# One new hand-written order of all operations, and tap products that take the two halves of the array in turn, in a state-space and MLP kernel

## The chip, the cores and the metric

The kernel runs on one core of a Trainium2 chip. Its engines are TensorE (PE in the profile, with its weight loads as PEld), VectorE (DVE), ScalarE (ACT), GpSimd (POOL) and SyncE (SP), which here only issues transfers. The metric is the device time of one execution in microseconds. Where several runs are given, their median counts.

## The reference

One sequence of 2048 positions and 512 channels goes through a long convolution and then through an MLP, each behind a layer norm and with a residual. Cut to what matters:

```python
dt = jnp.exp(log_dt)[:, None]
A = A_re + 1j * A_im; Bc = B_re + 1j * B_im; Cc = C_re + 1j * C_im
P = jnp.exp((dt * A)[:, :, None] * l[None, None, :])          # 512 channels, 128 states, 2048 taps
K = jnp.einsum("dn,dnl,dn->dl", Cc, P, dt * Bc).real
...
y = irfft(rfft(pad(u)) * rfft(pad(K)))[:L] + u * Dskip        # the convolution, by channel
h = x + y                                                     # u is the normed x
h2 = h + (gelu(layernorm(layernorm(h)) @ w1 + b1) @ w2 + b2)  # 512 -> 1376 -> 512
```

The tap index `l` is rounded to bfloat16, so that only some of its values are different from one another in the upper part of the range.

## The kernel before

**The filter.** The 2048 taps of K are made from two tables: a table A for 20 offsets and a table B for 33 multiples of eight, each of them with a real and an imaginary part, for 128 states (the partitions) and 512 channels in four blocks c of 128. The exponentials come from ACT (L793 for B, L991 for A), the sines and cosines from ACT too (L1026 for B, L1063 for A), with angles that PE adds up in PSUM (L1018, L1058, L1061), and DVE multiplies the two (L1036, L1043, L1068). Then `kgen` sums over the states on PE: **the tap products, L1092**. A product has 128 rows, 52 weight columns (two channels of 20 offsets with a gap of 12) and 66 moving columns (two channels of 33). For each step `i` there are four: `Ar` by `Br` and `Ai` by `Bi`, which add up in the same place of PSUM, for t = 0, in the left half of the array's columns (tile position (0, 0), output partitions from 0), and for t = 1, in the right half ((0, 64), partitions from 64). Each block has 32 steps, so there are 512 tap products in all. They read both tables with a step of four elements (`free(..., [[4, ...]])`). A copy from PSUM (`evac`) follows each group of 14 or 4 steps.

**The convolution and the MLP.** Further products on PE turn the taps and the input into a spectrum: `kspec` and `kspec1` (L1120, L1145), `austage` (L946) on the normed input, `fstage` (L967, of which `xspec` for the second half of the sequence is followed by a sum on DVE, L971), `ktail` and `klate` (L1166, L1187). `inverse` multiplies spectra on DVE (L1235) and goes back with PE (L1245), a copy, and a transposing transfer. `tail` adds the residual and does the norms (L1319, L1322, L1323, L1334), and `mlp` has the two matrix products (L1362 with its gelu on ACT in L1364, L1378 with the sum and the residual on DVE in L1380), for four quarters of the sequence. Each finished tile of the output leaves in two transfers from L632, and the very last tile in the program is split in two pieces of 256 columns.

**What sets the order.** Nothing is scheduled when the program is built. `add` records every operation with the engines that it may run on and what it depends on. `ORDER` (L292) is a list of 914 numbers, found beforehand by a search: each is twice the operation's index, plus one where it runs on the second of its possible engines. `Sched.run` (L390) walks the list, takes the eight PSUM slots as the string `SLOTS` says, and emits the operations in that order on each engine's queue, and each engine works its queue from the front. `evac` (L616 on ACT, L618 on DVE) is the main operation that may go to either engine; the row scaling by a norm (L931, L933; L1334, L1336) is another. A transfer may be issued by SP or ACT. A negative number in the list stands for a filler: four matmuls of 128 by 128 with the identity (L1451), into a free PSUM slot. The search used a cost for each operation; the one that stands in the code for a tap step is `add("PE", 0.064 * (hi - lo), ...)`, in microseconds.

Of the kernel before, what the change touches and what calls it, by code (L numbers as in the profile page):

```python
# [275 lines left out]
class VS(V):  # L276
# [13 lines left out]
LAG = {"PE": 0.12, "ACT": 0.20, "DVE": 0.14, "POOL": 0.15, "SP": 0.15}  # L290
OWN = {"PE": 0.0, "ACT": 0.17, "DVE": 0.11, "POOL": 0.1, "SP": 0.0}
ORDER = [  # L292
# [35 lines left out]
]  # L328
SLOTS = "0124626046204620462406220246200626224606446426424602606426042060242042604206246240264024604620406240245651620426262341302560134076205472541326036260721452042067563414307136506437056253104574107423"


TURN = 450000
# [108 lines left out]
def kernel(ctx, tc, A_u, A_A_re, A_A_im, A_B_re, A_B_im, A_C_re, A_C_im, A_log_dt, A_Dskip,  # L441
# [36 lines left out]
    def pst(p, dt=f32):  # L478
        a = banks[:, 512 * p.slot:512 * (p.slot + p.n)]
        return a if dt == f32 else a.bitcast(dt)  # L480
# [76 lines left out]
    def free(off, dims):  # L557

        a = ar[:, 0:1]
        return bass.AP(a.tensor, a.offset + off, [list(a.ap[0])] + dims)  # L560
# [515 lines left out]
    def kgen(c, pr):  # L1076
# [3 lines left out]
        for grp in KIS:  # L1080
            S.pr = pr + 0.01 * KIS.index(grp)
            p = Ps(n=len(grp))
            first = True
            for nb, (i0, n) in enumerate(grp):
                for lo, hi in ((0, n // 2), (n // 2, n)):
                    def fn(e, p=p, nb=nb, i0=i0, lo=lo, hi=hi):
                        for i in range(lo, hi):
                            for t in range(2):
                                q, f = 16 * t + 2 * ((i0 + i) // 4), (i0 + i) % 4
                                o = pst(p)[64 * t:64 * t + 32 + NA, 512 * nb + 2 * NB * i:512 * nb + 2 * NB * i + 2 * NB]  # L1090
                                for ta, tb in ((Ar, Br), (Ai, Bi)):
                                    pe.matmul(o, lhsT=free(ta.lo // 2 + q * 4 * NP_ + f, [[4, NP_ + NA]]), rhs=free(tb.lo // 2 + q * 4 * NB + f, [[4, 2 * NB]]), start=ta is Ar, stop=ta is Ai, tile_position=(0, 64 * t))  # L1092
                    add("PE", 0.064 * (hi - lo), fn, r=[Ar, Br, Ai, Bi], w=[p], new=[p] if first else [])
                    first = False
            i0, n = grp[0]
            N = len(grp)

            def ofn(i0=i0, n=n, N=N):
                return ks().rearrange("p z k i -> p (z k) i")[:, :, i0:i0 + n * N].rearrange("p q (b i) -> p q b i", b=N)

            def ifn(p=p, n=n, N=N):
                return pst(p).rearrange("p (b q) -> p b q", b=N)[:, :, 0:2 * NB * n].rearrange("p b (i q) -> p q b i", q=2 * NB)
            evac(ofn, ifn, 2 * NB * n * N, [p], [kg])
# [397 lines left out]
```

## Time and profile before

| | |
|---|---|
| median of 3 runs | 230.77 us (230.6 to 230.82) |
| the profiled execution | 230.71 us, its span 228.9 us |
| busy in the span: PE, PE's weight loads | 196.2 us (86%), 113.6 us (50%) |
| busy in the span: DVE, ACT, POOL | 173.5 us (76%), 164.4 us (72%), 14.6 us (6%) |
| instructions | 6859 |
| chain that ended last, by engine | PE 53%, ACT 26%, DVE 10%, DMA 4%, issue 4% |

The profile is of one execution, so the working is made against 230.71 us, of which 1.81 us lie outside the span. The two largest groups on PE are the matrix products of the MLP (L1362 40.1 us and L1378 39.8 us busy), and the tap products have 18.3 us. Busy time of PE counts a matmul from its start to its modelled end, so overlapping and waiting matmuls both look busy; starts that follow one another tell more.

### The profile page before, as it was taken

How to read it: one execution, taken by the hardware profiler on the slowest of the kernel's cores; microseconds unless marked ns; L12 is line 12 of the kernel's file. 1: busy time of each engine (PE TensorE's matmuls, PEld its weight loads, DVE VectorE, ACT ScalarE, POOL GpSimd, SP SyncE). 2: the span in 40 equal slices, each digit the busy share in tenths (PEclk: the TensorE clock that was granted, in tenths of full speed). 3: DMA queues.
4: the chain of work that ended last, by engine and by line, in shares of the span. 5: the costliest groups of instructions: out<-in, count | busy, mean ns of one | idle time of the engine just before them, and what ended most of it. 6: DMA issues, size and time to landing. Idle time of an engine off the chain costs nothing.

```text
span 228.9 us, 6859 instructions
## 1 busy us (share of the span) xinstructions
PE 196.2 (86%) x2974; PEld 113.6 (50%) x2981; DVE 173.5 (76%) x279; ACT 164.4 (72%) x203; POOL 14.6 (6%) x26
## 2 busy tenths in 40 slices
PE   7113886776999899999999769999999999999993
PEld 4102752233874479756566446654444434444452
DVE  7999778999897995779899989899957467113022
ACT  4999999999888997998997598593325405803800
POOL 2000300300010001200000030300000101000000
PEclk9999999999999999999999999999999999999998
DMA  5970191153006955486698991019340142051202
GB/s 154 191 145 6 53 234 41 51 159 127 6 3 118 227 145 146 131 180 158 175 243 164 258 227 67 3 33 218 72 93 21 29 101 69 11 126 44 63 21 70
DMA packets 43159, 25.09 MB, mean 110 GB/s; under 512 B 30197, under 2 KB 40697, under 8 KB 43130
## 3 DMA queue, kind: packets, MB, share of 16 engines
q1 hardware_dynamic: 41576, 22.72, 44.2%
q10 hardware_dynamic: 1554, 1.93, 2.7%
q8 instruction: 23, 0.38, 0.7%
q14 instruction: 6, 0.05, 0.1%
HBM read 14.13 MB, written 5.28 MB: 85 GB/s over the span
## 4 chain that ended last, share of the span: by engine, by line
PE 53%; ACT 26%; DVE 10%; DMA 4%; issue 4%; POOL 1%; ACTq 0%; SPq 0%; DVEq 0%; POOLq 0%
PE ps L1362 17%; PE ps L1378 17%; ACT ar L616 8%; PE ps L1092 7%; ACT ar L793 7%; ACT ar L1063 5%; ACT ar L991 4%; PE ps L1245 4%; DVE ar L1235 2%; DMA HL_d<-ar 2%; PE ps L946 2%; DMA ar<-AKc_d 2%; DVE ar L971 1%; DVE ar L1068 1%; ACT ar L701 1%
## 5 line engine op out<-in xcount | busy, mean ns | idle before, releaser
L616 ACT CAST ar<-ps 128x1024 bf16<-128x1024 f32 (+3 forms) x73 | 62.4, 917 | 10.8 <-PE ps L1245 5.3
L1364 ACT ACTIVATE ar<-ps,ar 128x512 bf16<-128x512 f32 (+1 forms) x44 | 27.6, 685 | 34.1 <-PE ps L1362 28.6
L1362 PE MATMUL ps<-ar 128*128 128x512 bf16 (+1 forms) x176 | 40.1, 379 | 0.1
L1378 PE MATMUL ps<-ar 128*128 128x512 bf16 (+3 forms) x181 | 39.8, 366 | 0.3
L1380 DVE TENSOR_TENSOR ar<-ps,ar 128x512 bf16<-128x512 f32 (+1 forms) x17 | 10.6, 652 | 26.7 <-issue 19.7
L1378 PEld LDWEIGHTS <-ar 128*128 128x128 bf16 (+1 forms) x187 | 17.9, 98 | 19.7 <-issue 0.7
L1362 PEld LDWEIGHTS <-ar 128*128 128x128 bf16 (+1 forms) x176 | 17.3, 100 | 20.2 <-issue 0.5
L618 DVE CAST ar<-ps 128x1024 bf16<-128x1024 f32 (+4 forms) x18 | 19.5, 1091 | 6.6 <-PE ps L1092 2.5
L1235 DVE TENSOR_TENSOR ar<-ar 128x2048 bf16<-128x2048 bf16 x20 | 24.0, 1218 | 0.5 <-ACT ar L616 0.3
L1245 PE MATMUL ps<-ar 64*128 64x128 bf16 x672 | 21.5, 216 | 1.9 <-DVE ar L1235 1.5
L1245 PEld LDWEIGHTS <-ar 64*128 64x128 bf16 x672 | 19.1, 94 | 6.5 <-issue 3.2
L1063 ACT ACTIVATE ar<-ps 128x1024 bf16<-128x1024 int16 x20 | 19.5, 1037 | 1.6 <-PE ps L1061 1.4
L1092 PE MATMUL ps<-ar 128*52 128x66 bf16 x512 | 18.3, 242 | 0.4 <-DVE ar L1068 0.4
L689 POOL TENSOR_TENSOR ar<-ar 128x4 f32<-128x4 f32 (+1 forms) x6 | 9.5, 1577 | 143.3 <-DVE ar L694 104.6
L1092 PEld LDWEIGHTS <-ar 128*52 128x52 bf16 x512 | 16.8, 128 | 2.7 <-issue 1.8
L946 PE MATMUL ps<-ar 128*32 128x512 bf16 x256 | 16.4, 381 | 1.0 <-DVE ar L931 0.9
L1026 ACT ACTIVATE ar<-ps 128x1024 bf16<-128x1024 int16 x16 | 15.9, 1035 | 0.4 <-PE ps L1018 0.3
L793 ACT ACTIVATE ar<-ar 128x1024 bf16<-128x1024 f32 x16 | 15.6, 1044 | 0.6 <-DVE ar L675 0.6
L1061 PE MATMUL ps<-ar 128*32 128x256 f16 (+1 forms) x256 | 12.9, 301 | 3.0 <-ACT ar L1063 2.8
L694 DVE SCALAR_TENSOR_TENSOR ar<-ar 128x4 f32<-128x4 f32 (+3 forms) x33 | 9.9, 305 | 6.4 <-POOL ar L689 5.4
L967 PE MATMUL ps<-ar 128*64 128x128 bf16 (+2 forms) x160 | 13.6, 298 | 0.9 <-ACT ar L616 0.9
L1068 DVE TENSOR_TENSOR ar<-ar 128x1024 bf16<-128x1024 bf16 x20 | 12.9, 682 | 0.6 <-ACT ar L1063 0.4
(83 smaller groups left out, 229.0 us busy)
## 6 DMA issues: line engine op xcount, KB each, us to landing
ar<-in_A_u_dram SPq DMA_DIRECT2D x16, 128.0 KB
ar<-in_A_u_dram SPq DMA_DIRECT2D x8, 256.0 KB
out_dram<-ar SPq DMA_DIRECT2D x30, 64.0 KB
ar<-in_B_w_dram SPq DMA_DIRECT2D x3, 344.0 KB
AK_d<-ar SPq DMA_DIRECT2D x2, 512.0 KB
AKc_d<-ar SPq DMA_DIRECT2D x4, 256.0 KB
ar<-tab_TP SPq DMA_DIRECT2D x1, 768.0 KB
ar<-AKc_d SPq DMA_DIRECT2D x3, 256.0 KB
```

The source lines that it names most:

```text
L616: act.copy(out_fn(), in_fn())
L618: dve.tensor_copy(out_fn(), in_fn())
L793: add("ACT", c_act(1024) + 0.03, lambda e, e0=e0: act.activation(free(EB0 // 2 + 4 * (16 - e0), [[8 * e0, 2], [4 * NB, NCH * CW // 4], [1, ...
L946: pe.matmul(pst(p)[32 * j:32 * j + 32, 512 * z:512 * z + 512], lhsT=BX.ap()[:, f0 + z, 16 - 16 * c:48 - 16 * c], rhs=src[2 * j + c].ap(), ...
L1026: add("ACT", c_act(1024), lambda e, p=p, sc=sc, cs=cs: act.activation(sc[cs].ap().rearrange("p c e d -> p (c e d)").rearrange("p (x e f) - ...
L1063: add("ACT", c_act(1024), lambda e, sc=sc: act.activation(sc.ap().rearrange("p z a b -> p (z a b)").rearrange("p (x a f) -> p a x f", a=4, ...
L1092: pe.matmul(o, lhsT=free(ta.lo // 2 + q * 4 * NP_ + f, [[4, NP_ + NA]]), rhs=free(tb.lo // 2 + q * 4 * NB + f, [[4, 2 * NB]]), start=ta is ...
L1235: dve.tensor_tensor(pq.ap().rearrange("p n d -> p (n d)"), a, b_, ALU.mult)
L1245: pe.matmul(pst(p)[:, 512 * h + 128 * k:512 * h + 128 * k + 128], lhsT=q.ap()[rows, x, :], rhs=TP[w].ap()[rows, f0 // 2 + k, :], start=(n ...
L1362: pe.matmul(pst(p)[:fs], lhsT=w1s[dc].ap()[:, fc * P:fc * P + fs], rhs=ybuf.ap().rearrange("p (t c) k -> p c t k", c=4)[:, dc], start=(dc ...
L1364: add("ACT", c_act(512, 1), lambda e, p=p, fc=fc, fs=fs: act.activation(hT.ap()[:fs, fc, :], pst(p)[:fs], ACT.Gelu_apprx_tanh, bias=b1_sb. ...
L1378: pe.matmul(pst(p)[:, c0:c1], lhsT=hT.ap()[:fs, fc, 128 * t:128 * t + 128], rhs=w2s[fc].ap()[:fs, c0:c1], start=(fc == 0), stop=(fc == NFC ...
```

## The change

Three things are changed, and the set of operations stays as it is: the same 914 operations with the same work and the same dependencies.

1. `ORDER` and `SLOTS` are replaced. (One row of the table stands for all.)
2. One filler, `-4`, stands in the new list: four matmuls with the identity into slot 3, between the transposed copies of L840 and the products of L865.
3. In `kgen`, the loop over the two halves is now inside the loop over the real and the imaginary part: the products go left, right, left, right where they went left, left, right, right.

```diff
 ORDER = [
-    2, 0, 52, 4, 58, 54, 56, 50, 62, 154, 6, 64, 66, 68, 74, 82, 8, 102, 104, 12, 10, 136, 194, 14, 140, 106, 88, 108, 16, 24, 32, 118, 100, 60, 28,
...
+    52, 0, 54, 6, 8, 2, 4, 10, 50, 64, 102, 62, 154, 12, 66, 68, 82, 76, 136, 98, 140, 70, 282, 104, 106, 86, 16, 78, 192, 14, 138, -4, 108, 118, 92,
...
                     def fn(e, p=p, nb=nb, i0=i0, lo=lo, hi=hi):
                         for i in range(lo, hi):
-                            for t in range(2):
-                                q, f = 16 * t + 2 * ((i0 + i) // 4), (i0 + i) % 4
-                                o = pst(p)[64 * t:64 * t + 32 + NA, 512 * nb + 2 * NB * i:512 * nb + 2 * NB * i + 2 * NB]
-                                for ta, tb in ((Ar, Br), (Ai, Bi)):
-                                    pe.matmul(o, lhsT=free(ta.lo // 2 + q * 4 * NP_ + f, [[4, NP_ + NA]]), rhs=free(tb.lo // 2 + q * 4 * NB + f, [[4, 2 * NB]]), start=ta is Ar, stop=ta is Ai, tile_position=(0, 64 * t))
+                            for ta, tb in ((Ar, Br), (Ai, Bi)):
+                                for t in range(2):
+                                    q, f = 16 * t + 2 * ((i0 + i) // 4), (i0 + i) % 4
+                                    o = pst(p)[64 * t:64 * t + 32 + NA, 512 * nb + 2 * NB * i:512 * nb + 2 * NB * i + 2 * NB]
+                                    pe.matmul(o, lhsT=free(ta.lo // 2 + q * 4 * NP_ + f, [[4, NP_ + NA]]), rhs=free(tb.lo // 2 + q * 4 * NB + f, [[4, 2 * NB]]), start=ta is Ar, stop=ta is Ai, tile_position=(0, 64 * t), skip_group_check=True)
                     add("PE", 0.064 * (hi - lo), fn, r=[Ar, Br, Ai, Bi], w=[p], new=[p] if first else [])
```

The order of the instructions moves on every engine. Three places matter for what follows.

**ACT, at the end of the sines of table A for the blocks c = 2 and 3** (L1063; `ps` is PSUM, `ar` the one large SBUF tile). The rows `128x66x14` and `128x66x4` are the copies of tap products, 14 or 4 steps each. Before:

```order
L1063 ACTIVATE ar<-ps 128x4x64x4 x4
L616 CAST ar<-ps 128x1024
L1063 ACTIVATE ar<-ps 128x4x64x4
L616 CAST ar<-ps 128x1024
L616 CAST ar<-ps 64x2x9x32
L1063 ACTIVATE ar<-ps 128x4x64x4
L616 CAST ar<-ps 128x1024 x4
L616 CAST ar<-ps 128x66x14
```

Now:

```order
L616 CAST ar<-ps 64x2x9x32
L1063 ACTIVATE ar<-ps 128x4x64x4
L616 CAST ar<-ps 128x1024 x2
L1063 ACTIVATE ar<-ps 128x4x64x4
L616 CAST ar<-ps 128x1024
L1063 ACTIVATE ar<-ps 128x4x64x4
L616 CAST ar<-ps 128x66x14
L1063 ACTIVATE ar<-ps 128x4x64x4
L616 CAST ar<-ps 128x66x14
L616 CAST ar<-ps 128x66x4
```

The first copy of block 2's tap products stood behind the last sine and four other copies; now it stands ahead of the last sine, so that block 2's tap products are on PE before block 3's sines are done. On PE, eight of the 16 `austage` and `xspec` groups of the first half of the sequence stood before the very first tap product; now eleven do.

**DVE, from the scaling of the second half's rows (L931) to the first products of `inverse` (L1235).** Before:

```order
L931 TENSOR_SCALAR ar<-ar 128x512 x2
L618 CAST ar<-ps 128x2x8x32
L931 TENSOR_SCALAR ar<-ar 128x512 x4
L1235 TENSOR_TENSOR ar<-ar 128x2048
L618 CAST ar<-ps 128x4x2x128
```

Now:

```order
L931 TENSOR_SCALAR ar<-ar 128x512
L618 CAST ar<-ps 128x66x14
L618 CAST ar<-ps 128x66x4
L1104 TENSOR_TENSOR ar<-ar 128x2x32
L1235 TENSOR_TENSOR ar<-ar 128x2048
L618 CAST ar<-ps 64x2x9x32
L618 CAST ar<-ps 128x1024
```

Copies of tap products that ACT did there are DVE's now. Over the list up to the first product of the MLP, DVE has 24 evacuations where it had 18, and ACT 69 where it had 75. Of DVE's six more, four are of 128x1024, one is of 128x924, and the sixth is the balance of smaller ones. DVE gives up one L931, two L1323 and one L1334 by the same point, which ACT does or which come later.

**SP, the last transfers of the program** (64 rows of the output each). Before:

```order
L632 DMA out_dram<-ar 64x512 x16
L632 DMA out_dram<-ar 64x256
L632 DMA out_dram<-ar 64x512 x2
L632 DMA out_dram<-ar 64x256
```

Now:

```order
L632 DMA out_dram<-ar 64x512 x12
L632 DMA out_dram<-ar 64x256
L632 DMA out_dram<-ar 64x512 x4
L632 DMA out_dram<-ar 64x256
L632 DMA out_dram<-ar 64x512 x2
```

The tile that is finished last was the second 256-column piece, whose two transfers left one from SP and one from ACT; now it is a whole tile of 512 columns, and both of its transfers leave from SP, one behind the other.

More of the change, by code (lines that the diff above doesn't have):

```diff
@@ L292 @@
 ORDER = [
[35 rows of a table removed]
[35 rows of a table added]
 ]
-SLOTS = "0124626046204620462406220246200626224606446426424602606426042060242042604206246240264024604620406240245651620426262341302560134076205472541326036260721452042067563414307136506437056253104574107423"
+SLOTS = "0124602642046204620240600602402624606041624020402062062046240240624026404062402460462024024062460260462102406710223421367242604132470176354620021601043072547124356403401576471540234614020321756474"
 TURN = 450000
```

68 rows, old and new, of the table ORDER are left out of this document.

## The prediction

> **What bounds the kernel now.** I read the stages first: the busy time of each engine in windows cut where the chain of waits changes its engine. Columns: the stretch, its length, then PE, its weight loads, DVE, ACT and POOL, busy us with counts.
>
> ```profile
> 0.00:119.30 119.30, 94.52 (x2046) 60.29 (x2048) 105.13 (x168) 109.96 (x126) 8.76 (x22) 1.00 0.54 128
> ...
> 25.00:47.00 22.00, 16.74 (x342) 9.29 (x338) 18.48 (x35) 21.93 (x24) 4.12 (x8) 1.00 0.39 99
> 47.00:57.00 10.00, 7.66 (x166) 3.81 (x154) 9.62 (x14) 9.52 (x11) 0.00 (x0) 1.00 0.48 152
> 57.00:69.40 12.40, 12.33 (x340) 9.72 (x344) 11.19 (x16) 10.84 (x13) 0.89 (x2) 1.00 0.02 4
> 69.40:80.00 10.60, 9.51 (x200) 4.75 (x196) 9.44 (x14) 10.05 (x12) 0.00 (x0) 1.00 0.94 182
> 80.00:94.50 14.50, 14.48 (x380) 11.98 (x378) 10.97 (x26) 12.57 (x16) 2.16 (x2) 1.00 0.48 134
> 94.50:119.30 24.80, 24.17 (x556) 14.88 (x557) 22.35 (x30) 23.16 (x28) 0.00 (x0) 1.00 0.80 190
> 119.30:140.70 21.40, 17.44 (x404) 12.79 (x400) 20.41 (x32) 16.62 (x22) 1.93 (x1) 1.00 0.86 198
> 140.70:225.40 84.70, 84.20 (x535) 40.50 (x539) 47.51 (x81) 37.84 (x56) 3.94 (x3) 1.00 0.30 63
> ```
>
> From 140.7, where the first product of the MLP starts, PE is busy 84.20 of 84.70 us: from there the end is fixed by PE's own work. So the question is when the MLP starts, and what stands behind 225.4. Ahead of 140.7 no one engine is the bound. ACT is full from 25 to 47, and DVE from 119.3 on. In between, the chain of waits (start, us, what) changes hands:
>
> ```profile
> 57.07 2.33 PE ps L1092 x66
> ...
> 69.47 1.03 ACT ar L1063
> ...
> 85.11 4.16 PE ps L1092 x120
> ...
> 94.53 0.59 ACT ar L616
> ```
>
> From 57 to 69.4 and from 80 to 94.5 it lies on PE, mostly on tap products; between them it lies on the sines of blocks 2 and 3 on ACT, and PE waits. Who waits for the taps says the list of waits (us in total, times, longest):
>
> ```profile
> DVE ar L618 <- PE ps L1092: 2.5, 2, 1.5
> ACT ar L616 <- PE ps L1092: 2.0, 4, 1.0
> DVE ar L618 <- PE ps L1145: 1.7, 1, 1.7
> ```
>
> **The turned tap products: nothing.** Do the halves already work at once? I looked at short windows of L1092 alone, where the count is of matmuls in flight, then of L967, whose 128-column products go left and right by turns in the program, and of L1254, whose products use the whole array.
>
> ```profile
> 57.06:57.08 0.02, 0.01 (x2) 0.01 (x2) 1.00 0.00 0
> 57.13:57.15 0.02, 0.02 (x4) 0.02 (x5) 1.00 0.00 0
> ...
> 57.06:59.40 2.34, 2.33 (x68) 2.16 (x68) 1.00 0.03 7
> ...
> L1092 PE MATMUL ps<-ar 128*52 128x66 bf16 x512 | 18.3, 242 | 0.4 <-DVE ar L1068 0.4
> ```
>
> ```profile
> 105.60:105.62 0.02, 0.02 (x2) 0.02 (x4) 1.00 0.61 218
> 105.62:105.64 0.02, 0.02 (x4) 0.02 (x6) 1.00 0.58 218
> ```
>
> ```profile
> 122.00 0.68 PE L1254 MATMUL ps<-ar 128*128 128x128 bf16 x9 [0.19 <-ACT ar L616]
> ...
> L1254 PE MATMUL ps<-ar 128*128 128x128 bf16 x16 | 1.1, 220 | 0.2 <-ACT ar L616 0.2
> ```
>
> Products on one and the same tile start one by one: L1254's nine in 0.68 us, (0.68 - 0.22) / 8 = 57 ns apart, never two within 20 ns. Taps start two within 20 ns, then two more by 57.13 to 57.15, some 65 ns later, and L967 likewise goes from two in flight to four. In the program the first two taps are both left ones, so I read the pair as one left and one right product: the array serves each half from its own queue and already overlaps them. Their rate, less the last one's own 0.24, is (2.33 - 0.24) / 67 = 31.2 ns a product, so each half takes 62 ns for 66 columns. What is slow is then each half by itself; the loads speak for the reading with a step of four elements as the cause:
>
> ```profile
> L1092 PEld LDWEIGHTS <-ar 128*52 128x52 bf16 x512 | 16.8, 128 | 2.7 <-issue 1.8 <-DVE ar L1068 0.6
> L967 PEld LDWEIGHTS <-ar 128*64 128x64 bf16 x160 | 6.9, 110 | 5.0 <-issue 3.3
> ```
>
> 52 stepped columns load in 128 ns, 64 plain ones in 110. Turning the order changes no reading, so I take 0. The bound below: the nearest row of products in turn,
>
> ```profile
> 122.99:125.10 2.11, 1.96 (x64) 1.79 (x64) 1.00 0.40 94
> ...
> L1245 PE MATMUL ps<-ar 64*128 64x128 bf16 x672 | 21.5, 216 | 1.9 <-DVE ar L1235 1.5 <-ACT ar L616 0.4
> ```
>
> L1245, has (1.96 - 0.22) / 63 = 27.6 ns a product: 512 x 3.6 = 1.8 us less PE work. A loss I exclude: L967 and L1245 pay nothing for turning.
>
> [...]
>
> **The new order, up to the MLP.** Two moves take PE work out of the stretches where PE is the chain. Three more groups of `austage` and `xspec` stand ahead of the first tap product, in 47 to 57, where PE has 2.3 us idle; and block 2's 128 tap products (128 x 31.2 = 4.0 us) are ready for PE before the last sines, where PE waits. So the copies that wait late for PE's results come sooner: I count DVE's waits for L1092 and L1145, 2.5 + 1.7 = 4.2 us, as gone. A third: DVE has one more early evacuation, which can fill its hole in 25 to 47 (22.0 - 18.48 = 3.5 us idle). The rows of these:
>
> ```profile
> L618 DVE CAST ar<-ps 128x1024 bf16<-128x1024 f32 x10 | 12.0, 1219 | 2.4 <-ACT ar L991 1.2 <-PE ps L967 0.9 <-PE ps L1120 0.3
> L618 DVE CAST ar<-ps 128x924 bf16<-128x924 f32 x3 | 3.4, 1118 | 2.5 <-PE ps L1092 2.5
> L618 DVE CAST ar<-ps 128x512 bf16<-128x512 f32 x2 | 1.4, 692 | 1.7 <-PE ps L1145 1.7
> L931 DVE TENSOR_SCALAR ar<-ar 128x512 bf16<-128x512 bf16 x16 | 5.6, 406 | 0.1
> L1323 DVE BATCH_NORM_STATS2 ar<-ps 128x6 f32<-128x512 f32 x4 | 2.5, 680 | 0.0
> L1334 DVE TENSOR_SCALAR ar<-ps,ar 128x512 bf16<-128x512 f32 x2 | 1.5, 804 | 0.0
> ```
>
> That gives 4.2 + 1.2 = 5.4 us less idle on DVE. Against it stands what DVE takes over from ACT: four copies of 1219, one of 1118 and a balance of about 0.4 make 6.4 us, less the scalings and statistics that it gives up (0.41 + 2 x 0.68 + 0.80 and two small ones of some 0.15: 2.9): 3.5 us more by the start of the MLP. Net 3.5 - 5.4 = **-1.9 us**. The cost is laid on DVE because it has the least air in 119.3 to 140.7 (20.41 of 21.40); ACT, with 16.62, gives those copies up, and takes the load of the gelu table earlier, under 1.3 us that it can bear.
>
> The ends of this term: DVE is idle 9.7 us between 47 and 140.7 (0.38 + 1.21 + 1.16 + 3.53 + 2.45 + 0.99). If all of it went, and the early copy filled its hole too, the term were 3.5 - 9.7 - 1.2 = -7.4; if none went, +3.5. I stay near the named waits, since the rest of DVE's idle is spread over waits under 1.5 us.
>
> **The filler and SP's queue: nothing.** Four matmuls in front of L865:
>
> ```profile
> PE ps L865 <- DVE ar L675: 9.4, 2, 8.7
> ...
> L840 PE MATMUL ps<-ar 128*128 128x128 bf16 x16 | 2.1, 285 | 0.0
> ...
> SPq L1261 <- DVE ar L1334: 24.9, 2, 15.2
> ```
>
> L865 waits 9.4 us for DVE there. L840's sixteen of the same size take (2.1 - 0.285) / 15 = 121 ns each, so the filler is 0.5 us, which it would cost if that wait were gone. The transfers and transposes that change places on SP wait longest for DVE's results (24.9 us for the two transposes of L1261), not for a place in the queue; up to the last ones I cost them at 0. One that waits for a late result would hold those behind it, up to the 15.2 us of the longest such wait; that belongs to the slower rival.
>
> **The end.** The last instructions before:
>
> ```profile
> 225.39 0.42 DVE L1380 TENSOR_TENSOR ar<-ps,ar 128x256 bf16<-128x256 f32 x1 [0.52 <-PE ps L1378]
> ...
> 225.42 1.23 SPq L632 DMA_DIRECT2D out_dram<-ar  x2
> ...
> L1380 DVE TENSOR_TENSOR ar<-ps,ar 128x512 bf16<-128x512 f32 x15 | 9.7, 683 | 24.3 <-issue 19.7 <-PE ps L1378 4.4 <-DMA out_dram<-ar 0.2
> ```
>
> SP issues a transfer in 1.23 / 2 = 0.6 us. The last sum took 0.42 us, and its transfer waited until SP was done with the one before, so the second issue ended 1.26 us after the sum's start. Now the sum takes 0.68 and two issues follow on one queue: 0.68 + 2 x 0.61 = 1.90. That is **+0.64 us**, with nothing to hide it; between +0.26 (only the sum) and +0.9.
>
> **Sum:** 230.71 - 1.9 + 0.64 = 229.45, say **229.5 us**. The profiled execution is within 0.06 of the median, 230.77.
>
> **The rivals.**
>
> *The halves do not overlap before* (0.14). Then turning halves the taps: 512 x 15.6 = 8.0 us less on PE between 57 and 94.5. For it: L1245 streams 128 columns in 2 x 27.6 = 55 ns a half, by which 66 would take 28.5, near the 31.2; against it: the paired starts. PE leaves the chain there, and DVE becomes the bound; of its other 9.7 - 4.2 = 5.5 us idle half would go, so 229.5 - 2.75 = 226.7.
>
> *DVE becomes the bound* (0.27), the case on the slower side. In 94.5 to 140.7 it is busy 42.76 of 46.2 us, and the new list puts copies of tap products there just ahead of L1235. If they stand in its queue ahead of products that PE, ACT and a transposing transfer wait for, DVE's idle only changes place. It decides where less than 3.5 + 0.64 = 4.1 of the hoped 5.4 us goes. With half of the 4.2 left, 3.5 - 3.3 + 0.64 = +0.8, 231.5; with all of it, 3.5 - 1.2 + 0.64 = +2.9, 233.6. I take 231.9.
>
> *It comes out even* (0.13): the list was sought with costs that differ from the chip's elsewhere, and the middle wins no more than the end loses: 230.7. PE's 84.2 us behind 140.7 stand in both lists.
>
> **How the numbers follow.** My forecast has 0.46, with its own range 228.2 to 230.5. The predicted time is 229.5. For 8 in 10 the range reaches into the first rival and into the slower one: 226.9 to 232.5. About 0.2% is what a measurement of this kernel tells from no change (230.3 to 231.2). Faster by more: 0.42 + 0.14 + 0.03 = 0.59; within: 0.04 + 0.03 + 0.06 = 0.13; slower: 0.24 + 0.04 = 0.28.
>
> **What would show it.** Tap rate: L1092 in 31 ns a product, starting two by two (my reading), or 16 (first rival). DVE's waits for L1092 and L1145 nearly gone, and its idle up to the MLP's first product down from 15.2 us to about 10; if it stays over 11, the second rival. The first L1362 at about 138.8. From it to PE's last matmul 84.7 us as before. Behind the last matmul 4.1 us in place of 3.5. I am wrong if the MLP's own stretch changes, which I took as fixed.

## The result and the profile after

| | before | changed |
|---|---|---|
| median, us | 230.75 (5 runs, 230.6 to 230.82) | 232.77 (5 runs, 232.09 to 233.24) |
| profiled execution, its span, us | 230.71, 228.9 | 232.77, 231.0 |
| first product of the MLP (L1362), us | 140.70 | 141.98 |
| PE's last matmul ends, us | 225.4 | 226.7 |

The changed kernel is slower: ratio 1.007, 95% interval 1.0049 to 1.0091. That is outside the forecast range, on the other side of no change.

The first view cuts the program at the first product of the MLP and at PE's last matmul (columns as in the prediction). Before:

```profile
0.00:140.70 140.70, 111.96 (x2442) 73.08 (x2444) 125.54 (x199) 126.58 (x147) 10.69 (x23) 1.00 0.59 139
```

Changed:

```profile
0.00:141.98 141.98, 116.21 (x2447) 71.14 (x2448) 129.91 (x203) 124.55 (x144) 12.54 (x22) 0.98 0.52 130
141.98:226.72 84.74, 84.58 (x539) 40.37 (x539) 48.32 (x82) 35.23 (x53) 4.45 (x4) 1.00 0.34 75
```

The MLP's stretch is 84.74 us (84.70 before), and behind it 231.0 - 226.72 = 4.3 us follow instead of 3.5. So of the 2.1 us of span, 1.3 arise ahead of the MLP and 0.8 at the end. Ahead of the MLP, DVE works 129.91 - 125.54 = 4.4 us more and idles 12.1 us instead of 15.2: it idles less, but not by the 5.4 us that the forecast counted. And PE's granted clock, the column before the DMA share, was 1.00 before and is 0.98. Slices of four us show where. Before:

```profile
28.00:32.00 4.00, 3.14 (x84) 2.53 (x76) 3.17 (x10) 4.00 (x5) 0.90 (x2) 1.00 0.84 215
32.00:36.00 4.00, 3.42 (x66) 1.51 (x66) 2.35 (x2) 3.97 (x6) 0.00 (x0) 1.00 0.79 185
36.00:40.00 4.00, 2.58 (x66) 0.94 (x58) 3.73 (x7) 3.98 (x6) 0.00 (x0) 1.00 0.00 0
```

Changed:

```profile
28.00:32.00 4.00, 2.20 (x63) 1.42 (x53) 2.43 (x6) 4.00 (x5) 3.09 (x2) 1.00 0.74 238
32.00:36.00 4.00, 2.48 (x22) 0.98 (x25) 1.84 (x6) 3.97 (x5) 0.00 (x0) 0.61 0.14 32
36.00:40.00 4.00, 3.83 (x59) 1.18 (x51) 3.65 (x5) 1.11 (x3) 0.33 (x1) 0.54 0.01 2
...
32.00:33.00 1.00, 0.38 (x1) 0.09 (x1) 1.00 (x4) 1.00 (x3) 0.00 (x0) 0.93 0.50 111
33.00:39.00 6.00, 5.00 (x51) 1.68 (x50) 3.53 (x7) 3.14 (x5) 0.00 (x0) 0.50 0.02 4
39.00:40.00 1.00, 0.93 (x26) 0.39 (x24) 0.97 (x3) 0.94 (x2) 0.33 (x1) 0.66 0.00 0
```

Three things stand in these rows. PE's clock is half from 32.9 (0.93 in 32 to 33) to 39.7 (0.66 in 39 to 40). ACT, full before, is busy 1.11 of 4 us from 36 to 40. And POOL is busy 3.09 us in 28 to 32, where it had 0.90. The chain of waits there (start, us, what), before:

```profile
35.44 0.64 ACT ar L701
...
36.10 0.70 DVE ar L694
...
39.92 4.20 DMA HL_d<-ar
```

and changed:

```profile
35.37 0.64 ACT ar L701
...
36.32 1.23 DVE ar L618
...
38.92 0.70 DVE ar L694
...
42.74 4.62 DMA HL_d<-ar
```

Both lists are level up to the end of ACT's L701, at 36.0 us. Then DVE's steps to the HL transfer, from whose data the sines of the tables are made, begin at 38.92 instead of 36.10, because two copies (L618) of L946's products stand ahead of them and come late. The transfer leaves 2.8 us later, and the first tap product starts at 60.15 instead of 57.07. What holds the copies up is seen in the timeline of POOL, DVE and PE (start, us, engine, operation, and in brackets the wait ahead of it). Before:

```profile
26.79 1.95 POOL L689 TENSOR_TENSOR ar<-ar 128x8 f32<-128x8 f32 x1 [24.60 <-DVE ar L694]
```

Changed:

```profile
27.43 3.50 POOL L689 TENSOR_TENSOR ar<-ar 128x8 f32<-128x8 f32 x1 [8.05 <-DVE ar L694]
...
27.55 1.34 DVE L756 MEMSET ar<- 128x1536 f32 x1 [0.27 <-issue]
28.80 0.63 DVE L689 TENSOR_TENSOR ar<-ar 128x512 f32<-128x512 f32 x1
...
31.17 2.67 DVE L931 TENSOR_SCALAR ar<-ar 128x512 bf16<-128x512 bf16 x8
...
32.28 0.38 PE L946 MATMUL ps<-ar 128*32 128x512 bf16 x1 [1.21 <-ACT ar L991]
33.90 3.60 PE L946 MATMUL ps<-ar 128*32 128x512 bf16 x31 [1.24 <-DVE ar L931]
```

The same small operation on POOL, one step of the statistics of the layer norm, takes 3.50 us instead of 1.95, beside a memset of DVE that started at 2.86 us in the kernel before, ahead of all this. It also starts 0.64 us later, so that the scalings (L931), which need its result, come 2.2 us later in all (31.17 instead of 28.98). L946 needs the scalings, and PE waits twice, 1.21 and 1.24 us. The clock falls during the second wait, and 31 products then take 3.60 us. Which of these links carries the time is what the experiments had to tell.

### The profile page after: what moved, and what is told of

Read it like the earlier page. It is cut to its first block, busy times and chain, and to the rows that moved or that the text cites. A ratio compares the mean times of both kernels' runs of the same rounds, so it can differ in the third digit from the quotient of the medians.

```text
span 231.0 us, 6862 instructions
## 1 busy us (share of the span) xinstructions
PE 200.8 (87%) x2985; PEld 111.5 (48%) x2985; DVE 178.9 (77%) x285; ACT 159.8 (69%) x197; POOL 17.0 (7%) x26
## 3 DMA queue, kind: packets, MB, share of 16 engines
q1 hardware_dynamic: 41608, 22.89, 41.2%
## 4 chain that ended last, share of the span: by engine, by line
PE 56%; ACT 20%; DVE 11%; DMA 8%; issue 4%; POOL 0%; ACTq 0%; DVEq 0%; SPq 0%; POOLq 0%
PE ps L1378 17%; PE ps L1362 17%; ACT ar L793 7%; PE ps L1092 6%; ACT ar L616 5%; PE ps L1245 4%; ACT ar L991 4%; DVE ar L1235 3%; DMA AK_d<-ar 3%; ACT ar L1063 2%; PE ps L1061 2%; DMA HL_d<-ar 2%; DMA ar<-AK_d 2%; DVE ar L618 2%; DVE ar L971 2%
## 5 line engine op out<-in xcount | busy, mean ns | idle before, releaser
L616 ACT CAST ar<-ps 128x1024 bf16<-128x1024 f32 (+4 forms) x68 | 59.2, 921 | 18.3 <-PE ps L1245 8.5
L1378 PE MATMUL ps<-ar 128*128 128x512 bf16 (+3 forms) x187 | 41.2, 367 | 0.1
L1362 PE MATMUL ps<-ar 128*128 128x512 bf16 (+1 forms) x176 | 40.8, 379 | 0.0
L618 DVE CAST ar<-ps 128x1024 bf16<-128x1024 f32 (+5 forms) x23 | 24.7, 1079 | 3.6 <-ACT ar L701 2.5
L1362 PEld LDWEIGHTS <-ar 128*128 128x128 bf16 (+1 forms) x176 | 17.4, 100 | 20.1
L1235 DVE TENSOR_TENSOR ar<-ar 128x2048 bf16<-128x2048 bf16 x20 | 24.0, 1220 | 0.5 <-PE ps L1245 0.3
L946 PE MATMUL ps<-ar 128*32 128x512 bf16 x256 | 18.4, 411 | 2.9 <-DVE ar L931 1.2
L689 POOL TENSOR_TENSOR ar<-ar 128x4 f32<-128x4 f32 (+1 forms) x6 | 11.4, 1896 | 119.8 <-DVE ar L694 110.1
L1063 ACT ACTIVATE ar<-ps 128x1024 bf16<-128x1024 int16 x20 | 19.7, 1035 | 0.2
L1092 PE MATMUL ps<-ar 128*52 128x66 bf16 x512 | 18.6, 243 | 0.2 <-ACT ar L616 0.2
L1092 PEld LDWEIGHTS <-ar 128*52 128x52 bf16 x512 | 16.6, 129 | 3.1 <-issue 2.4
L967 PE MATMUL ps<-ar 128*64 128x512 bf16 (+2 forms) x160 | 14.4, 299 | 0.7 <-DVE ar L618 0.3
(87 smaller groups left out, 228.6 us busy)
```

What stands on the lines that cost most here:

```text
L616: act.copy(out_fn(), in_fn())
L618: dve.tensor_copy(out_fn(), in_fn())
L946: pe.matmul(pst(p)[32 * j:32 * j + 32, 512 * z:512 * z + 512], lhsT=BX.ap()[:, f0 + z, 16 - 16 * c:48 - 16 * c], rhs=src[2 * j + c].ap(), ...
L1063: add("ACT", c_act(1024), lambda e, sc=sc: act.activation(sc.ap().rearrange("p z a b -> p (z a b)").rearrange("p (x a f) -> p a x f", a=4, ...
L1235: dve.tensor_tensor(pq.ap().rearrange("p n d -> p (n d)"), a, b_, ALU.mult)
L1362: pe.matmul(pst(p)[:fs], lhsT=w1s[dc].ap()[:, fc * P:fc * P + fs], rhs=ybuf.ap().rearrange("p (t c) k -> p c t k", c=4)[:, dc], start=(dc ...
```

## The experiments

Ratios are to the kernel before, timed beside each run on the same chip; times are medians. The kernel before took 231.27 us beside e1 to e4, 230.82 beside e5 to e8, 230.83 beside e9 and e10 and 231.31 beside e11 and e12, so the ratios compare better than the times. "HL" is the issue of the HL transfer (42.02 us changed, 39.20 before), "MLP" the first L1362 (141.9 changed).

| run | what differs from the changed kernel | us | ratio, 95% interval | HL | MLP |
|---|---|---|---|---|---|
| e1_old_taps | taps in the old order | 232.33 | 1.0051 (1.0032 to 1.0070) | 41.7 | 141.4 |
| e2_evacs_act | two early copies on ACT | 231.95 | 1.0038 (1.0021 to 1.0055) | 39.1 | 141.9 |
| e3_warm | 8 fillers ahead of L946 | 232.75 | 1.0075 (1.0052 to 1.0098) | 41.2 | 141.9 |
| e10_warm4 | 4 fillers there | 232.01 | 1.0050 (1.0031 to 1.0068) | 41.2 | 142.0 |
| e4_memset_late | the memset behind L931 | 230.11 | 0.9957 (0.9941 to 0.9973) | 39.6 | 139.3 |
| e6_before_memset | (the kernel before, with the memset moved) | 232.17 | 1.0056 (1.0036 to 1.0076) | 40.1 | 141.5 |
| e5_memset_tail | e4, split tile last | 232.46 | 1.0071 (1.0050 to 1.0092) | 39.6 | 140.2 |
| e9_memset_tail2 | e4, split tile last, other order on SP | 230.78 | 0.9994 (0.9980 to 1.0008) | 39.6 | 139.2 |
| e11_memset_act_end | e4, last transfer on ACT | 229.80 | 0.9951 (0.9935 to 0.9967) | 40.2 | 139.8 |
| e12_pool_alone | e11, DVE's L689 moved too | 229.98 | 0.9949 (0.9934 to 0.9965) | 39.7 | 139.2 |

### The order of the taps

e1 puts the loop of `kgen` back; the new list stays.

```diff
-                            for ta, tb in ((Ar, Br), (Ai, Bi)):
-                                for t in range(2):
+                            for t in range(2):
+                                for ta, tb in ((Ar, Br), (Ai, Bi)):
```

> The changed kernel with the tap products in their old order (left, left, right, right). Theory 'the halves overlap either way': L1092 stays at 31 ns a product, first L1362 within 0.3 us of the changed kernel's 142.0 us, time 232 to 233.3 us like the changed kernel's 232.77. Rival 'the turn itself costs': the time falls by 0.5 us or more.

The time lies in the expected band, though the MLP started 0.5 us earlier, more than the 0.3 allowed. The intervals of e1 and of the changed kernel overlap. The 0.46 us by which the first tap came earlier (59.69 instead of 60.15) is there ahead of any tap product: behind 32 us, PE's half clock was shorter in this execution.

```profile
32.00:36.00 4.00, 2.48 (x25) 1.12 (x28) 1.85 (x7) 3.97 (x5) 0.00 (x0) 0.79 0.14 25
36.00:40.00 4.00, 3.41 (x63) 1.17 (x59) 3.97 (x5) 1.74 (x2) 0.66 (x1) 0.79 0.01 2
```

Twice 0.79 is 2 x 4 x 0.42 = 3.4 us of half clock, not 6.8. Two more runs tested the reading of the hardware behind "the turned tap products: nothing". In e7 the products of the right half are left out (`for t in range(1)`), so half of the tap sums is missing; in e8 all reads are of neighbouring elements, so the taps work on other data:

```diff
-lhsT=free(ta.lo // 2 + q * 4 * NP_ + f, [[4, NP_ + NA]]), rhs=free(tb.lo // 2 + q * 4 * NB + f, [[4, 2 * NB]])
+lhsT=free(ta.lo // 2 + q * 4 * NP_ + f, [[1, NP_ + NA]]), rhs=free(tb.lo // 2 + q * 4 * NB + f, [[1, 2 * NB]])
```

> The changed kernel without the tap products of the right half (256 instead of 512; half of the tap sums is left out). Theory 'each half has its own queue and takes 62 ns a product': the products that are left start 58 to 64 ns apart, so a group takes as long as before. Rival 'the halves take turns at 31 ns': 27 to 34 ns apart, and a group takes half of its time.

> The changed kernel with the tap products reading neighbouring elements instead of every fourth (other data, the same number of products, rows and columns). Theory 'the step of four is what makes a half slow': 66 columns take 28 to 33 ns a half, so 14 to 18 ns a product, loads of 52 columns near 100 to 110 instead of 128 ns, and the first group of taps takes 1.0 to 1.3 us instead of 2.36. Rival 'the length or the issue sets it': 31 ns a product stays.

The first group of taps in the changed kernel, as a window of L1092 alone (its length, matmuls and loads):

```profile
60.15:62.51 2.36, 2.36 (x68) 2.18 (x68) 1.00 0.03 7
```

and the loads of the whole line, from the groups:

```profile
L1092 PEld LDWEIGHTS <-ar 128*52 128x52 bf16 x512 | 16.6, 129 | 3.1 <-issue 2.4 <-DVE ar L1043 0.4 <-DVE ar L1068 0.3
```

The same window with the left half alone (e7):

```profile
59.21:61.50 2.29, 2.29 (x34) 2.13 (x34) 1.00 0.03 7
```

With plain reads (e8) the window of the second group, and then the groups of the line:

```profile
62.20:63.20 1.00, 0.86 (x44) 0.75 (x44) 1.00 0.00 0
```

```profile
L1092 PE MATMUL ps<-ar 128*52 128x66 bf16 x512 | 11.0, 195 | 0.9 <-ACT ar L616 0.8
L1092 PEld LDWEIGHTS <-ar 128*52 128x52 bf16 x512 | 9.5, 105 | 4.2 <-issue 4.1
```

(e7 took 231.39 us and e8 231.97, one run each.) Half as many products take as long: (2.29 - 0.24) / 33 = 62 ns each, against (2.36 - 0.24) / 67 = 32 ns with both halves. Plain reads take (0.86 - 0.195) / 43 = 15.5 ns a product, 31 ns a half, and a load 105 instead of 129 ns. (The first group of e8, from 60.06 us on, kept PE busy for 1.42 us, longer than the 1.0 to 1.3 expected; why is open.) So here the halves work side by side in either order (31.2 ns a product before, 32 now), and with the step of four each of them is half as fast (62 ns a product instead of 31). e8 changes the step of the weights and of the moving columns together; which of the two costs is not separated. And e8 says something on the price of the taps: they keep PE busy 11.0 instead of 18.6 us, yet its span, 230.2 us, is only 0.8 us shorter than the changed kernel's 231.0, at the same mean granted clock of 0.985. That is one run, but it gives no sign that faster taps alone would bring the 2.75 us that the first rival adds to the forecast.

### Copies, clock or memset

e2 gives DVE's two early copies to ACT; PE's order stays.

```diff
  DVE:  L931 TENSOR_SCALAR ar<-ar 128x512 x8
- DVE:  L618 CAST ar<-ps 128x1024
  DVE:  L677 TENSOR_SCALAR ar<-ar 128x512
- DVE:  L618 CAST ar<-ps 128x1024
  ACT:  L701 ACTIVATE ar<-ar 128x512
+ ACT:  L616 CAST ar<-ps 128x1024 x2
```

> The two early copies of austage results (L618, 36.32 and 37.79 us in the changed kernel), which stand on DVE ahead of the chain L694 to the HL transfer, go to ACT, which is idle there from 36.0 to 38.8. Theory A 'the copies hold up the HL chain': the HL transfer is issued at 39.9 instead of 42.0 to 42.7, the first tap product comes at 57.0 to 57.6 instead of 60.15, and the time falls by 1.5 to 2.9 us to 229.9 to 231.3. Theory B 'the half clock between 32.9 and 39.7 us is what costs': L1026 stays as late as it is, and the time falls by less than 0.7 us.

The HL transfer left at 39.1, even before the 39.9 of theory A, and the time hardly followed: it is 0.8 us under the changed kernel's, between the two bands, and the first tap product came at 60.31. ACT now waits for L946 itself (0.47 us ahead of its copy at 41.07), and PE met half clock a little later. A window of e2, and its first sine in the timeline:

```profile
40.00:44.00 4.00, 4.00 (x56) 0.99 (x48) 1.26 (x2) 2.79 (x4) 0.22 (x2) 0.67 0.39 70
```

```profile
50.98 1.12 ACT L1063 ACTIVATE ar<-ps 128x1024 bf16<-128x1024 int16 x1
```

PE is busy throughout, and ACT only 2.79 of 4 us. The first sine starts at 50.98, as late as in the changed kernel (50.88). Theory A alone falls: taken off DVE, the wait shows on ACT.

e3 adds eight fillers (32 products) on PE between the last L988 and the first L946, e10 four:

```diff
  PE:   L988 MATMUL ps<-ar 32x256
+ PE:   L1451 MATMUL ps<-ar 128x128 x32
  PE:   L946 MATMUL ps<-ar 32x512
```

> Eight fillers more (32 matmuls with the identity) between the last L988 and the first L946, where PE waits from 31.1 to 33.9 us. Theory B: the clock stays at 1.0, L946's first 32 products take 1.9 instead of 3.6 us, the HL transfer is issued 0.9 to 1.7 us earlier, the spread of the times (232.09 to 233.24) shrinks to 0.3 us, and the time falls to 231.3 to 231.9. Theory A: the same start of the copies, but they still stand ahead of the chain, so at most 1.2 us is gained. If the clock falls all the same, the wait of PE isn't its cause.

> The changed kernel with four fillers more (where the earlier run had eight). Theory B in its mended form 'the half clock costs about 1 us, and the run with eight fillers lost it again at a halt of PE's instructions at 95.1 us': the clock stays at 1.0, the HL transfer leaves near 41.2 instead of 42.0, no halt of 0.6 us in the tap products, first L1362 near 141.0 instead of 141.9, time 231.5 to 232.0. Rival 'the us is lost again in any case': first L1362 at 141.8 or later, time 232.5 to 233.

In both the clock stays whole there, HL leaves 0.9 us earlier (41.15), and the first tap starts at 59.2. That much is theory B. But neither starts the MLP earlier, and the time of e3 and its spread (232.24 to 233.79) are not what theory B expected. In e3 the timeline has PE halting inside a group of tap products, with no releaser named:

```profile
94.60 0.50 PE L1092 MATMUL ps<-ar 128*52 128x66 bf16 x10
95.68 0.63 PE L1092 MATMUL ps<-ar 128*52 128x66 bf16 x14 [0.58 <-issue]
```

In e10 no such halt stands in the taps, but the profiled execution, the slowest of its six (231.77 to 232.87), met half clock later, ahead of the MLP, as a window shows:

```profile
134.00:139.00 5.00, 4.55 (x75) 3.86 (x76) 4.83 (x8) 3.79 (x8) 0.52 (x1) 0.66 0.99 248
```

So the clock costs about 0.9 us up to the taps; what of it reaches the end is not settled by these two, whose intervals overlap that of the changed kernel, and the halt in e3 stays unexplained. Nor is the fall of the clock certain: e7, without a filler and with both waits of PE, kept its clock (1.0 over its span). Its group of L946 (busy us, mean ns, and the waits ahead, the same two of 1.2 us among them; the mean is 411 ns in the changed kernel):

```profile
L946 PE MATMUL ps<-ar 128*32 128x512 bf16 x256 | 16.7, 381 | 2.9 <-DVE ar L931 1.2 <-ACT ar L991 1.2 <-ACT ar L616 0.5
```

e4 moves one instruction of DVE:

```diff
  DVE:  L694 SCALAR_TENSOR_TENSOR ar<-ar 128x8 x2
- DVE:  L756 MEMSET ar 128x64x24
  DVE:  L689 TENSOR_TENSOR ar<-ar 128x512
  DVE:  L694 SCALAR_TENSOR_TENSOR ar<-ar 128x8
  DVE:  L931 TENSOR_SCALAR ar<-ar 128x512 x8
+ DVE:  L756 MEMSET ar 128x64x24
```

> The memset of 128x1536 (L756) on DVE, which in the changed kernel runs at 27.5 us beside POOL's L689, goes behind the last scaling L931. Theory C 'DVE's memset holds POOL up': L689 on POOL takes 1.9 to 2.1 us instead of 3.5, the scalings start at 29.5 instead of 31.2, the copies and the HL transfer come 0.9 to 1.6 us earlier, PE's wait is shorter and the clock may stay whole, time 231.0 to 232.0. Rival 'POOL's time is its own, or L689 on DVE with two inputs does it': 3.5 us stays, and the time is within 0.4 us of the changed kernel's.

This one move turns the result: 230.11 us, 0.43% below the kernel before, below the expected band. The timeline of e4, and then its windows:

```profile
27.43 1.96 POOL L689 TENSOR_TENSOR ar<-ar 128x8 f32<-128x8 f32 x1 [8.04 <-DVE ar L694]
...
29.62 2.68 DVE L931 TENSOR_SCALAR ar<-ar 128x512 bf16<-128x512 bf16 x8
```

```profile
32.00:36.00 4.00, 2.79 (x52) 1.75 (x51) 3.72 (x5) 3.97 (x5) 0.00 (x0) 1.00 0.25 53
36.00:40.00 4.00, 3.48 (x68) 1.35 (x68) 3.83 (x7) 4.00 (x5) 1.49 (x2) 1.00 0.02 4
...
0.00:139.36 139.36, 114.45 (x2447) 71.97 (x2448) 129.76 (x203) 124.51 (x144) 11.00 (x22) 1.00 0.54 133
```

POOL's step takes 1.96 us, the scalings start 1.55 us earlier, PE meets no half clock, ACT is full again, and the MLP starts 2.6 us earlier. HL leaves 2.4 us earlier, which is the 1.55 of POOL and the 0.9 of the clock. Over all runs, five of e4's six had a mean granted clock of 0.995 or more, and none of the changed kernel's five had more than 0.990. The reverse is e6, the kernel before with nothing moved but that memset, from DVE's start to the place beside POOL's L689.

> The kernel before, with nothing changed but that its second memset of 128x1536 on DVE (2.86 us) goes beside POOL's L689 (ahead of L689 of 128x512 on DVE). Theory C: POOL's L689 takes 3.3 to 3.6 us instead of 1.95, the scalings L931 come 1.3 to 1.7 us later, the HL transfer and the first tap product 0.5 to 2.5 us later, and the time is 0.5 to 2.0 us longer than before. Rival 'POOL's 3.5 us came from something else in the changed order': 1.95 us stays, the time within 0.3 us.

Its timeline on POOL:

```profile
26.80 3.50 POOL L689 TENSOR_TENSOR ar<-ar 128x8 f32<-128x8 f32 x1 [24.60 <-DVE ar L694]
```

3.50 us again, HL 0.9 us later, and 0.56% slower; its shortest run (231.66 us) is longer than the longest of the kernel before beside it (231.60). The memset's place is a cause by itself, in either list. (The page of e6 also has a granted clock of 0.7 in its slice from 132.2 to 137.9 us, of which the MLP's start may hold a part.) e12, on top of e11 below, also moves DVE's L689 of 128x512, which has two inputs in SBUF (0.68 us from 27.19 on in e4), behind the scalings.

> As the run before it, with DVE's L689 of 128x512 (two inputs from SBUF) moved behind the scalings too, so that DVE does nothing wide while POOL's L689 runs. Theory 'any wide DVE work there holds POOL up': POOL's L689 takes 1.0 to 1.3 us instead of 1.95 and the scalings start 0.6 to 0.9 us earlier. Rival 'the memset alone did': 1.9 to 2.0 us stays. The first L946 waits for ACT until 32.3 in either case, so the time moves by less than 0.3 us.

The same step on POOL in e12:

```profile
27.43 1.65 POOL L689 TENSOR_TENSOR ar<-ar 128x8 f32<-128x8 f32 x1 [8.05 <-DVE ar L694]
```

1.65 us instead of the 1.96 of e4, between the two expectations: that operation of DVE held POOL up by 0.3 us, the memset by 1.55 (3.50 to 1.95). The time moved by less than the intervals, as both expected.

### The end

e5 makes the split tile the last again, on top of e4, and e9 does so with the sums and transfers in the order in which they get done. e11 keeps the new order and changes one queue:

```diff
-dma("ACT" if h and len(cols_) == 2 else "SP",
+dma("ACT" if h and not_[0] >= 15 else "SP",
```

> The kernel with the late memset, and at its end the split tile is the last again: its two halves leave from SP and ACT. Theory 'the end costs what the prediction said': 0.6 us less than with the late memset alone, from PE's last matmul to the end 3.9 us instead of 4.7 (both from the start of the last matmul), 229.5 us, 0.7 to 0.9% below the kernel before. Rival 'the last transfers are bound by their landing': within 0.2 us of 230.1.

> As the kernel with the late memset and the split tile last, but the sums and transfers of the last five tiles leave in the order in which they get done, so that SP has no transfer waiting in front of finished ones. Theory 'the end costs what the prediction said, and the first try only failed by its order on SP': 3.7 to 4.1 us from the start of the last matmul to the end instead of 4.66 with the late memset alone and 6.9 in the first try, and where the clock stays whole 229.2 to 229.7 us. Rival 'the last transfers cost the same in any order': 4.6 us or more, 230.1 us.

> The kernel with the late memset, in which the last tile's lower transfer leaves from ACT, idle by then, instead of standing behind the other one on SP. Theory 'at the end SP's queue of issues decides, 0.6 us each': from the start of the last matmul to the end 4.0 to 4.2 us instead of 4.66, time 0.4 to 0.6 us under the late memset alone, 229.4 to 229.8 us, 0.5 to 0.7% below before. Rival 'the landing decides': 4.5 us or more.

SP's last issues in the timeline (start, us, count); the spans are 228.9 us before, 231.0 changed, 228.4 in e4, 231.6 in e5, 228.9 in e9 and 228.6 in e11. Before:

```profile
224.90 1.74 SPq L632 DMA_DIRECT2D out_dram<-ar  x3
```

Changed, and behind it the last row of its chain:

```profile
224.83 3.73 SPq L632 DMA_DIRECT2D out_dram<-ar  x5
```

```profile
226.74 0.69 DVE ar L1380
```

e4:

```profile
224.87 1.10 SPq L632 DMA_DIRECT2D out_dram<-ar  x2
```

e5:

```profile
224.86 4.44 SPq L632 DMA_DIRECT2D out_dram<-ar  x7
```

e9:

```profile
224.79 1.88 SPq L632 DMA_DIRECT2D out_dram<-ar  x3
```

e11, and the last row of its chain:

```profile
225.35 0.47 SPq L632 DMA_DIRECT2D out_dram<-ar  x1
```

```profile
224.63 0.69 DVE ar L1380
```

The span ends 2.2 to 2.4 us behind SP's last issue in the first five (before 226.64 to 228.9, e5 229.30 to 231.6, e9 226.67 to 228.9). So the end follows SP's queue in these five. Both attempts with the split tile last were misses: in e5 a transfer that waited stood at the head of SP, and seven issues followed one another; in e9 too many tiles were done in the last 2 us for one queue. (e5 also met half clock near 40 us, with 0.70 in 36 to 40 and 0.87 in 40 to 44: its MLP starts 0.9 us later than e4's.) e11 takes one issue off SP: from the last sum to the end 3.97 us instead of 4.25, 0.3 us of the hoped 0.6; SP's issue ends at 225.82 and the span 2.8 us later, so ACT's transfer or the landing decides now. (e11 also met a lower clock from 32 us on: the 32 products of L946 at 32.28 take 3.42 us, 1.98 in e4, and its MLP starts 0.5 us later than e4's.) e11 and e12, at 0.9951 and 0.9949, beat both kernels as e4 does, but their intervals overlap e4's.

## Why the prediction was wrong

**The turned tap products: nothing.** Right, and for the reason given: 62 ns a half with or without the other half, and the step of four as the cause (31 ns a half with plain reads). The first rival, halves that do not overlap, is excluded by e7. Of L967, which turns too, the trace of before has sixteen products of 128x128 in 0.64 us from 105.55 on: (0.64 - 0.22) / 15 = 28 ns each, 56 a half, next to L1254's 57 on the whole array.

**The new order, up to the MLP.** The waits that were counted went. DVE's for L1092 and L1145, 4.2 us before, are 0.5 us in the changed kernel's list of waits (us in total, times, longest):

```profile
DVE ar L618 <- ACT ar L701: 2.5, 1, 2.5
...
DVE ar L618 <- PE ps L1092: 0.5, 2, 0.3
```

Without the misplaced memset (e4), DVE's idle up to the MLP is 139.36 - 129.76 = 9.6 us, 5.6 less than before, where 5.4 were forecast. That the two agree so well is partly luck: in e4 DVE idles 5.9 us less behind 47 us, where 4.2 were counted, and 1.4 us less in 25 to 47, which the moved memset's 1.34 us alone would fill; but ahead of 25 us, where the memset used to be, it idles 1.75 us more, which was not counted. Its work is 4.2 us more, where 3.5 were forecast. So the order without the misplaced memset is worth -1.3 us rather than -1.9, and that part of the term was mis-sized by DVE's work.

**The step that failed** lies in the term of the new order, -1.9 us, at its third move: "DVE has one more early evacuation, which can fill its hole in 25 to 47". That hole was taken for free room, and what DVE moves within its own queue was put at nothing without being read; only what it takes over from ACT was. In the new list a memset stands in the hole, beside the one small operation of POOL on which the scalings wait. The first row above is that wait: it names ACT's L701, which ends at 36.0, but the copy waits until 36.3 for L946, which is late by way of L931 and POOL; in e4 the same copy starts at 33.92, ahead of the end of L701. The memset costs 1.55 us on POOL and, through PE's waits and the half clock behind them, 2.6 us at the start of the MLP (141.98 against 139.36 in e4). The -1.3 became +1.3. Some 0.9 of the 2.6 hang on the half clock, which is not the memset's alone: e7 did without it though the memset stood there, and e5 and e11 met it though the memset stood elsewhere.

**The filler and SP's queue: nothing.** No experiment took the filler out, but the trace of the changed kernel bears the reason out: its four matmuls end at 7.2 us, and PE then idles 8.86 us until L865 starts at 16.04. SP's queue up to the last transfers was not tested by itself.

**The end.** Forecast +0.64, 4.1 us behind the last matmul; measured 4.3 against 3.5, so +0.8, within its bounds of 0.26 and 0.9. The mechanism came about too. From the start of the last sum to the end it is 4.26 us (226.74 to 231.0) instead of 3.51 (225.39 to 228.9): the sum takes 0.69 instead of 0.42 us, from its end to the end of SP's last issue pass 1.13 instead of 0.83, and from there to the end of the span 2.44 instead of 2.26. That makes 0.27 + 0.30 + 0.18 = 0.75; the first two are the terms of the forecast, the third is the landing, which it left out. That the second issue on SP is worth some 0.3 us, e11 shows.

**The slower rival.** Its marker, an idle of DVE above 11 us, was met (12.1), but not its mechanism: the wait is not at the copies ahead of L1235, it is at 25 to 42 us. That its bounds (231.5 to 233.6) hold the time is luck; the predicted range, which ended at 232.5, was too short on that side because a hold-up on POOL and a fall of the clock were in none of the cases. MLP's stretch, fixed by forecast, stayed at 84.7 us.

Sum: 230.71 - 1.3 (order) + 2.6 (memset and half clock) + 0.8 (end) = 232.8, the measured 232.77. The first two terms are differences of the same three starts of the MLP (140.70, 139.36 and 141.98), so that the sum comes out shows that nothing is left over, not that the causes are right; for these stand e4 and e6.

## What to carry to other kernels

When a list is sought anew, read the moves of every engine against what its neighbours do at that moment, also those of work that changes neither engine nor size: here one memset of 1.34 us, moved into an idle stretch, cost more, with the half clock behind it (2.6 us), than the whole new order gained (1.3). An idle stretch is free only if the result on which the engine waits does not get later by filling it. And where an output goes through one queue, count its issues behind the last result (one less was worth 0.3 us in e11); a reordering that looks better by the size of the last tile can be worse by the queue, as e5 was with seven issues in 4.44 us.

## What the hardware showed

A memset on DVE, which reads nothing (1.34 us for 128x1536), made a power of 128x8 on POOL take 3.50 instead of 1.95 us, in two lists (the changed one and e6), and 1.96 once it was moved away (e4). DVE's L689 of 128x512, with two inputs, had a smaller effect on the same step: 1.96 to 1.65 us when it was moved too (e12).

In the changed kernel PE's clock fell to half (0.50 from 33 to 39 us) during the second of two waits of 1.21 and 1.24 us, with PE busy 2.20 of the 4 us from 28 to 32, and stayed there for 6.8 us. In three other profiles the mean clocks of two slices of 4 us come to 3.4 us of half clock: 0.79 and 0.79 from 32 on in e1, 0.91 and 0.67 from 36 on in e2, 0.70 and 0.87 from 36 on in e5. Which run meets half clock, and where, differs between executions of nearly the same program: e7, with the same two waits of PE, met none, so no threshold can be read from these traces. It is not the changed kernel's alone either. The kernel before spread by 0.22 us in the five runs of the first table, but by 1.1 us in the 15 beside e1 to e4, where its two runs at a granted clock of 1.0 took 230.65 and 230.73 us and its four at 0.989 took 231.55 to 231.71.
